# Batch 1's second FFN product by seven half products; first products in pairs; some mask products on GpSimd

## The chip, the cores and the metric

The kernel runs on one core of one Trainium2 chip. A core has five engines with queues of their own: TensorE (PE, with its weight loads PEld), VectorE (DVE), ScalarE (ACT), GpSimd (POOL) and SyncE (SP). Each works off its instructions in the order in which they were written and waits on semaphores for the others. The metric is the device time of one execution in microseconds (us). Before the change the median of three runs is 285.59 us (285.23 to 285.65); the execution that the profile shows took 285.7 us, of which its span is 284.0 us.

## What is computed

Local-global attention over 8 batches of 8 heads (head size 64), then a feed-forward block over all tokens. Each batch has 512 local and 32 global tokens.

```python
s_g = scale * q_g @ concat(k_g, k_l).T          # 32 global queries see everything
out_g = softmax(s_g) @ concat(v_g, v_l)
s_l = concat(scale * q_l @ k_g.T, where(|i - j| <= 32, scale * q_l @ k_l.T, -1e9))
out_l = softmax(s_l) @ concat(v_g, v_l)
x = concat(out_g, out_l) as (4352 tokens, 512)
h = x @ w_in            # 512 -> 2048
g = h * sigmoid(1.702 * h)
out = g @ w_out         # 2048 -> 512
```

The inputs are float32; the kernel computes with bf16 operands and float32 sums.

## The kernel before

**Work units.** A batch's 512 local tokens are a block `xL[i]`, i = 0 to 7. The global rows of all batches are gathered in `xG`, a last block of 256 rows. Two "quads" per batch, called a and c, hold four heads each on the four 32-row strips of TensorE. For each quad the code has these steps:

- `Tk`, `Tq` (L512, L316): VectorE turns the loaded k and q into the layout for TensorE; `kcopy`, `qcopy` (L504, L507) make a second, shifted copy of a part; `ext` (L538 to L545, four small copies, parts 0 to 3) puts the global rows beside them.
- `S(rnd)` (L560): TensorE makes half of the scores, round 0 or 1, into a pair of double banks that all scores share (`spair`). `X(rnd)` (L571): ScalarE takes the exponential, in two instructions of about 1000 elements. `M(rnd)` (L576): the product with the band mask, on VectorE or GpSimd.
- `U(0)`, `U(1)`, `U(2)` (L586), `Gm` (L597); together `UG`: TensorE makes the softmax sums, the two halves of the local output, and the global output, each in a bank of the pool `psP` of four banks.
- `R` (L462 to L466): VectorE turns and inverts the sums; `XL(0)`, `XL(1)` (L471) scale the local output into `xL`. `G` (L476 to L479, three small instructions) does the same for the global output into `xG`.

**First product** (512 to 2048): the block `fc`, 0 to 15, is 128 columns of `w_in`; `h_mm` makes it with four matmuls of 512 columns (L617), ScalarE's gelu (L622) takes it from its bank to `gT`. `h_step` is one `fc`. From batch 3 on `HPair(i, g)` makes the two blocks of one g (fc 2g and 2g + 1) as a 2 by 2 block product with seven half products in place of eight (L699, 14 matmuls of 256 columns), with sums of the weights (`h_weight_sums`, L660) and of the tokens (`x_sums`, L673, L674). Its steps are `m3` (a ScalarE copy of the first product), `z`, `zm`, `sub`, `add` (VectorE, L707 to L716), `inner` and `outer` (gelu).

**Second product** (2048 to 512): for batches 0 and 1 by `o_mm`, 64 matmuls of 512 columns per batch (L731). From batch 2 on by two `Pair`s per batch, seven half products each of eight matmuls of 256 columns (L800), with sums of the weights (`weight_sums`, L745: numbers 0, 3 and 4 into tiles of their own, 1 and 2 in place of parts of `w_out_sb`) and of `gT` (`g_sums`, L770, L773). Its steps have the same names as those of `HPair`: `m3` (ACT, L113), `z`, `zm`, `sub`, `add` (VectorE, L812 to L825), `evict` (ACT, L113), `store` (SP's DMAs, L838).

**Order.** The order of the work is written out by hand, engine by engine. The loop over i does, for each batch, the first product of batch i (`h_some(i)` from i = 3), and then a phase (`phase_o1` for i = 1, `phase_o(i)` for 2 to 6) in which the second product of batch i lies among the scores, exponentials, masks and outputs of batch i + 1 and the first scores of quad a of batch i + 2 (called a2, its sister c2). At the end stand the last second products and the block of the global rows. ScalarE has to load a table when it goes from gelu to exponential and back (`exp_table`, `gelu_table`, or before the first such instruction). Loads of q, k (`load`, L81, L82) and v (`load_v`, L98, L100) are issued by GpSimd's queue, the stores of results by SP's.

In `phase_o1` before the change, quad a's M(0) and M(1), c's and a2's are all on VectorE; in `phase_o` only a2's M(0) is on GpSimd.

## Time and profile before

| | |
|---|---|
| median of three runs | 285.59 us (285.23 to 285.65) |
| profiled execution | 285.7 us; its span 284.0 us |
| PE busy | 277.0 us, 98% of the span |
| DVE busy | 228.9 us, 81% |
| ACT busy | 182.1 us, 64% |
| POOL busy | 107.1 us, 38% |
| PE clock granted | 1.00 |
| L617 (first product, 128x512 matmuls) | 97.0 us busy for 432 |
| L731 (second product of batches 0 and 1) | 29.5 us busy for 128 |

The busy time of a matmul overlaps with that of the next, so rates are read from the start of one group to the start of the next. The 40 digits of an engine in the page are its busy tenths in slices of 7.1 us. The stages, by the start of their first matmul: first product of batch 0 from 17.7 us, second product of batch 0 from 31.7, first product of batch 1 from 51.0, `phase_o1` from 65.9, first product of batch 2 from 85.8, `phase_o(2)` from 99.7, `h_some(3)` from 117.3, `phase_o(3)` from 131.0, `h_some(4)` from 148.6, `phase_o(4)` from 162.3, `h_some(5)` from 180.2, `phase_o(5)` from 194.0, `h_some(6)` from 211.7, `phase_o(6)` from 225.3, `h_some(7)` from 241.7, the rest from 255.5.

### The profile page before, as it was taken

Reading aid. Unit: us, or ns where it says so; the run is one execution under the profiler, and the core shown is the slowest. Engines: PE = TensorE matmul, PEld = TensorE weight load, DVE = VectorE, ACT = ScalarE, POOL = GpSimd, SP = SyncE. Lnnn points to the kernel's source line nnn. Section 1 sums busy time; section 2 is a strip of 40 time slices with the busy share of each in tenths; the row PEclk is TensorE's granted clock in tenths of the full one; section 3 lists DMA queues with packets and bytes.
Section 4 is the critical chain, followed back from the end, with each engine's and each line's share of the span. In section 5 each row is a group of like instructions: output and inputs, shape, how many; then the busy total and the mean of one; then the engine's idle time right before and its main releaser. Section 6 shows DMA issues by size and latency. Waiting matters only on the chain.

```text
span 284.0 us, 9001 instructions
## 1 busy us (share of the span) xinstructions
PE 277.0 (98%) x3763; PEld 182.3 (64%) x3763; DVE 228.9 (81%) x518; ACT 182.1 (64%) x299; POOL 107.1 (38%) x172
## 2 busy tenths in 40 slices
PE   7899999999999999999999999999999999999994
PEld 6454445544554488746885588647875589558884
DVE  7584458986689899999989998999988898586452
ACT  4858757577778784688457873788459761873331
POOL 8993550765946001990079302960041000000001
PEclk9999999999999999999999999999999999999999
DMA  7999995899999801795039802980022003200223
GB/s 208 159 195 210 203 162 77 148 217 144 170 165 183 151 2 48 78 177 91 14 69 163 150 5 68 84 97 3 21 58 74 2 3 76 74 3 0 58 54 112
DMA packets 59352, 28.24 MB, mean 99 GB/s; under 512 B 47472, under 2 KB 49776, under 8 KB 59312
## 3 DMA queue, kind: packets, MB, share of 16 engines
q0 software_dynamic: 51760, 17.83, 56.2%
q1 hardware_dynamic: 7120, 9.18, 11.7%
q8 instruction: 29, 0.48, 0.7%
q10 hardware_dynamic: 432, 0.66, 0.7%
q14 instruction: 11, 0.09, 0.1%
HBM read 36.31 MB, written 8.91 MB: 159 GB/s over the span
## 4 chain that ended last, share of the span: by engine, by line
PE 86%; DVE 7%; DMA 2%; issue 1%; POOL 1%; ACT 1%; DVEq 0%; POOLq 0%; ACTq 0%
PE hp L617 31%; PE px L800 12%; PE op L731 10%; PE py L800 9%; PE x L800 6%; PE s L560 5%; PE ov L586 5%; PE s L699 3%; PE s L617 3%; DMA rq<-in_q_l_dram 2%; DVE gs L773 2%; DVE gs L770 1%; DVE xL L471 1%; DVE kT L512 1%; PE og L597 1%
## 5 line engine op out<-in xcount | busy, mean ns | idle before, releaser
L617 PE MATMUL hp<-xL,w_in_sb 128*128 128x512 bf16 x432 | 97.0, 379 | 0.2 <-DVE xL L471 0.2
L617 PEld LDWEIGHTS <-w_in_sb 128*128 128x128 bf16 x528 | 51.4, 98 | 51.8 <-issue 0.4
L622 ACT ACTIVATE gT<-hp 128x512 bf16<-128x512 f32 x108 | 62.7, 600 | 17.1 <-PE hp L617 16.6
L571 ACT ACTIVATE e<-s 128x1016 bf16<-128x1016 f32 (+1 forms) x56 | 53.3, 1003 | 25.7 <-PE s L560 25.7
L800 PEld LDWEIGHTS <-gs 128*128 128x128 bf16 x480 | 46.2, 98 | 6.6
L576 POOL TENSOR_TENSOR e<-e,mask 128x1760 bf16<-128x1760 bf16 x4 | 13.3, 3320 | 70.0 <-ACT e L571 70.0
L98 POOL DMA_DIRECT2D v<-in_v_l_dram x40 | 31.1, 780 | 13.6 <-PE og L597 3.8
L773 DVE TENSOR_TENSOR gs<-gT 128x512 bf16<-128x512 bf16 (+1 forms) x87 | 31.6, 398 | 3.3 <-ACT gT L622 3.3
L800 PE MATMUL py<-wsum,gs 128*128 128x256 bf16 x240 | 30.3, 273 | 0.0
L731 PE MATMUL op<-w_out_sb,gT 128*128 128x512 bf16 x128 | 29.5, 380 | 0.0
L576 DVE TENSOR_TENSOR e<-e,mask 128x1712 bf16<-128x1712 bf16 (+1 forms) x24 | 25.2, 1049 | 3.5 <-ACT e L571 3.5
L512 DVE STREAM_TRANSPOSE kT<-rk 128x512 f32<-128x512 f32 x14 | 14.5, 1037 | 12.6 <-DMA rk<-in_k_l_dram 12.6
L833 POOL DMA_DIRECT2D out_dram<-ob x2 | 1.2, 596 | 60.5 <-ACT ob L113 60.3
L731 PEld LDWEIGHTS <-gT 128*128 128x128 bf16 x128 | 11.8, 98 | 14.0
L800 PEld LDWEIGHTS <-gT 128*128 128x128 bf16 x192 | 18.0, 98 | 3.0
L800 PE MATMUL px<-w_out_sb,gT 128*128 128x256 bf16 x160 | 19.2, 273 | 0.1
L800 PE MATMUL px<-w_out_sb,gs 128*128 128x256 bf16 x160 | 19.1, 273 | 0.0
L471 DVE TENSOR_TENSOR xL<-ov,rs 128x512 bf16<-128x512 f32 x27 | 17.9, 686 | 1.0 <-PE ov L438 0.3
L113 ACT ACTIVATE ob<-px 128x512 f32<-128x512 f32 x10 | 6.0, 599 | 19.3 <-DVE zz L822 19.3
L770 DVE TENSOR_TENSOR gs<-gT 128x1024 bf16<-128x1024 bf16 (+1 forms) x29 | 17.2, 598 | 0.0
L560 PEld LDWEIGHTS <-kT 32*128 32x128 bf16 x672 | 12.5, 93 | 6.8 <-issue 5.7
L100 POOL DMA_DIRECT2D v<-in_v_g_dram x24 | 14.0, 585 | 2.2 <-DMA rq<-in_q_l_dram 1.7
(176 smaller groups left out, 429.3 us busy)
## 6 DMA issues: line engine op xcount, KB each, us to landing
out_dram<-ob SPq DMA_DIRECT2D x128, 64.0 KB, 2.7
rq<-in_q_l_dram POOLq DMA_DIRECT2D x5, 512.0 KB, 8.2
rk<-in_k_l_dram POOLq DMA_DIRECT2D x5, 512.0 KB, 10.0
v<-in_v_l_dram POOLq DMA_DIRECT2D x24, 96.0 KB, 4.8
w_in_sb<-in_moe_w_in_dram POOLq DMA_DIRECT2D x8, 256.0 KB, 6.9
w_out_sb<-in_moe_w_out_dram POOLq DMA_DIRECT2D x4, 512.0 KB, 10.1
rk<-in_k_l_dram POOLq DMA_DIRECT2D x5, 256.0 KB, 7.8
rq<-in_q_l_dram POOLq DMA_DIRECT2D x5, 256.0 KB, 7.2
```

What stands on the lines that cost most here:

```text
L98: nc.gpsimd.dma_start(out=vt[0:n, hs, c, :D], in_=vs[FIRST[c] : FIRST[c] + n, hs])
L471: nc.vector.tensor_mul(self.x[:, 2 * self.u + h, :], self.st[1 + h], self.st["rs"])
L512: nc.vector.transpose(flat[:, 0:Sl].rearrange("p (r t) -> p t r", t=16), loaded[self.b][0][:, self.u].bitcast(F32))
L560: nc.tensor.matmul(bank(self.ps, j)[:, at : at + n], lhsT=self.k[p, KEYS[c] : KEYS[c] + 128, e], rhs=qs[p, :, :, e], start=(e == 0), stop= ...
L571: nc.scalar.activation(self.E[rnd][:, 2 * i : 2 * i + 2, :n], self.ps[i][:, :, :n], AF.Exp, scale=scale)
L576: eng.tensor_mul(e, e, mask[:, rnd : rnd + 1, :n].to_broadcast([128, 4, n]))
L617: nc.tensor.matmul(hp[:, : width(i)], lhsT=w_in_c[:, fc // 4, kc, fc % 4 // 2, :, fc % 2], rhs=(xL[i] if i < B else xG)[:, kc, :], start=( ...
L622: nc.scalar.activation(out_, in_, AF.Gelu_apprx_sigmoid)
L731: nc.tensor.matmul(op, lhsT=gTs[i][:, fc, tci * 128 : tci * 128 + 128], rhs=w_out_sb[:, fc, :], start=(first and fc == 4 * f4), stop=(fc = ...
L770: nc.vector.tensor_tensor(sums[i][2][:, g, :n], t[:, g, 0, :n], t[:, g, 1, :n], ALU.add)
L773: nc.vector.tensor_tensor(sums[i][k][:, g, : n // 2], x[:, g], y[:, g], op)
L800: nc.tensor.matmul(out_, lhsT=lv[:, g, tt * 128 : tt * 128 + 128], rhs=rv[:, g, :], start=(g == 0 and k in ((1, 3, 4, 6) if self.apart els ...
```

## The change

- **Second product of batch 1.** `phase_o1` is rewritten: two `Pair`s (112 matmuls of 256 columns) in place of `o_mm` (64 of 512). The order of quads' steps among them is new. The whole second product now stands ahead of c's outputs; the first matmuls of batch 2's first product (`h_two`, new) follow after c's `UG`, a2's S(0), and among them a2's S(1).
- **Weight sums.** 0, 3 and 4 are made in four quarters each, behind the DMAs of `w_out`, during batch 0; 1 and 2 at the start of batch 1's first product. `g_sums` for batch 1 are new.
- **First product in pairs.** For batches 3 to 6 `HPair` makes g = 1 and 2 in one go (28 matmuls of 256 columns for four blocks; its vector and scalar steps are twice as wide). `h_weight_sums(2)` is new.
- **Masks.** On GpSimd are now also c's M(0) and a2's M(0) of `phase_o1`, and a2's M(1) of `phase_o(2)`, `(3)` and `(4)`.
- **Global output.** `G` is split: `keep_og` copies the bank to a tile by ScalarE, `GG` scales both quads together later on VectorE.
- **Copies.** a2's `kcopy`, `qcopy`, `ext` go to ScalarE (for batch 2 among the gelus, else inside the phase); c2's `Tk` and `Tq` stand in `phase_o` ahead of `x_sums`. S(0) of batch 2 stands one `fc` later.
- **Loads.** `load_v` of batch i + 3 is cut in two, ahead of and behind a2's M(0); `load(i + 3)` goes from the end of the phase to `h_some`, behind a2's M(1).
- **`g_sums`** of the third kind (k = 2) for g = 4 to 7 stand inside `phase_o(3)` to `(6)` in one instruction.

```diff
...
-    def load_v(b, hs=slice(0, 8)):
+    def load_v(b, hs=slice(0, 8), chunks=range(5)):
         if b == 2:
             nc.gpsimd.memset(v_view(b, 5)[:, :, :, :, D:], 1.0)
         vt = v_view(b, 5).rearrange("p u j c d -> p (u j) c d")
         vs, vg = (x[b].rearrange("h s d -> s h d") for x in (v_l, v_g))
-        for c in range(5):
+        for c in chunks:
             n = 128 if c == 2 else 96
             nc.gpsimd.dma_start(out=vt[0:n, hs, c, :D], in_=vs[FIRST[c] : FIRST[c] + n, hs])
...
+    def keep_og(q, ogs):
+        on_act(ogs[:, q.u], q.st["og"][:, : D + 2])
+
+    def GG(b, ogs):
+        rg = att.tile([128, 2, 1], F32, name="rgg")
+        nc.vector.reciprocal(rg, ogs[:, :, D : D + 1])
+        xg = att.tile([128, 2, D], BF16, name="xgg")
+        nc.vector.tensor_mul(xg, ogs[:, :, :D], rg.to_broadcast([128, 2, D]))
+        for u in range(2):
+            nc.vector.transpose(xG_by_row[:, 2 * u : 2 * u + 2, b // 4, :, b % 4],
+                                xg[:, u].rearrange("p (d h) -> p h d", h=2))
+
...
         h_act(i, fc, hp)
 
     w_h = {g: [w_in_c[:, g // 2, 2 * k : 2 * k + 2, g % 2, :, e] for e in range(2) for k in range(2)]
-           for g in (1, 4)}
-    w_s = early.bitcast(BF16).rearrange("p a b -> p (a b)")[:, : 5 * 2 * 256].rearrange(
-        "p (k u c m) -> p k u c m", k=5, u=2, c=2)
+           for g in (1, 2, 4)}
+    w_s = early.bitcast(BF16).rearrange("p a b -> p (a b)")[:, : 5 * 3 * 256].rearrange(
+        "p (k u c m) -> p k u c m", k=5, u=3, c=2)
     wh = {g: [w_s[:, k, u] for k in range(5)] for u, g in enumerate(w_h)}
...
-    def weight_sums(*ks):
+    def weight_sums(*ks, g=slice(0, FC // 2)):
         for k in ks:
             x, y, op = ((b11, b22, ALU.add), (b12, b22, ALU.subtract), (b21, b11, ALU.subtract),
                         (b11, b12, ALU.add), (b21, b22, ALU.add))[k]
-            nc.vector.tensor_tensor(wsum[k], x, y, op)
+            nc.vector.tensor_tensor(wsum[k][:, g], x[:, g], y[:, g], op)
...
         if fc == 4:
             h_weight_sums(1)
         if fc == 12:
+            h_weight_sums(2)
             h_weight_sums(4)
+    weight_sums(0, 3, 4, g=slice(2, 4))
+    weight_sums(0, 3, 4, g=slice(0, 2))
...
+    weight_sums(0, 3, 4, g=slice(4, 6))
...
+    weight_sums(0, 3, 4, g=slice(6, 8))
...
-    a.G()
-    c.G()
-    weight_sums(0, 3, 4)
-    nq[2][0].Tk()
-    nq[2][0].Tq()
-    transpose_g(4, 6)
-    nq[2][0].ext()
+    ogs = att.tile([128, 2, D + 2], F32, name="ogs", bufs=1)
+    keep_og(a, ogs)
+    keep_og(c, ogs)
+    weight_sums(1, 2)
+    GG(1, ogs)
...
     a, c = nq[2]
     for fc in range(FC):
-        if fc == 11:
-            c.Tk(False)
-            c.Tq(False)
-            c.ext((0, 1, 2))
-            c.kcopy(nc.vector.tensor_copy)
-            c.ext((3,))
-            c.qcopy(nc.vector.tensor_copy)
...
         elif fc >= 8:
             h_step(1, fc)
+        if fc == 3:
+            g_sums(1, 0, 2)
+            a.Tk(False)
+            a.Tq(False)
+            transpose_g(4, 6)
+        if fc == 6:
+            g_sums(1, 2, 4)
+            c.Tk(False)
+            c.Tq(False)
+            c.kcopy(nc.vector.tensor_copy)
+            c.qcopy(nc.vector.tensor_copy)
+            c.ext()
+        if fc == 8:
+            a.kcopy(on_act)
+        if fc == 9:
+            a.qcopy(on_act)
+        if 10 <= fc < 14:
+            a.ext((fc - 10,), on_act)
         if fc == 13:
+            g_sums(1, 4, 7, (0, 1))
+        if fc == 14:
             a.S(0)
-
-    def o_parts(i, *parts):
...
     def phase_o1():
         a, c = nq[2]
         a2, c2 = quads_of(3)
-        a2.T()
-        transpose_g(6, 8)
-        a2.ext()
+        p0, p1 = Pair(1, 0), Pair(1, 1)
+        ogs = att.tile([128, 2, D + 2], F32, name="ogs", bufs=1)
+        load_g(8, NQ)
+        load(4)
+        load_v(3, chunks=(0, 1))
+        g_sums(1, 7, 8, (0, 1))
+        p0.mm(3, 4)
+        p0.m3()
         a.X(0)
-        a.M(0)
-        loads_after(1)
-        o_parts(1, 0, 1, 2, 3, 4)
+        p0.z()
+        g_sums(1, 4, 8, (2, 3))
+        p0.mm(1, 6)
+        p0.zm()
+        p0.mm(5)
         a.S(1)
         a.X(1)
+        a2.Tk(False)
+        a.M(0)
+        p0.mm(2)
+        p0.sub()
+        p0.evict()
+        p0.mm(7)
         a.M(1)
-        o_parts(1, 5, 6, 7)
         c.S(0)
         c.X(0)
-        a.UG()
+        p0.add()
+        p0.store()
+        ov = [pbank("ov"), pbank("ov")]
+        p1.mm(3)
+        a.U(0, ov[0])
+        a.U(1, ov[1])
+        a.U(2)
         a.R()
-        c.M(0)
-        o_parts(1, 8)
+        p1.mm(4)
+        a.Gm()
+        p1.m3()
+        keep_og(a, ogs)
+        a2.kcopy(on_act)
+        c.M(0, nc.gpsimd)
+        load_v(3, chunks=(2, 3, 4))
+        a.XL(0)
+        p1.z()
+        a.XL(1)
         c.S(1)
         c.X(1)
-        a.XL(0)
-        a.XL(1)
-        a.G()
+        p1.mm(1, 6)
+        p1.zm()
+        a2.Tq(False)
+        transpose_g(6, 8)
         c.M(1)
-        o_parts(1, 9, 10, 11)
+        p1.mm(5, 2)
+        p1.sub()
+        p1.evict()
+        a2.qcopy(on_act)
+        a2.ext(copy=on_act)
+        p1.mm(7)
+        p1.add()
+        p1.store()
+        ov = [pbank(n) for n in ("ov", "og", "ov", "ov")]
+        c.U(0, ov[0])
+        c.U(1, ov[2])
+        c.U(2, ov[3])
+        c.Gm(ov[1])
         a2.S(0)
         a2.X(0)
-        c.UG()
-        loads_after(2)
         c.R()
-        a2.M(0)
+        keep_og(c, ogs)
+        a2.M(0, nc.gpsimd)
         c.XL(0)
         c.XL(1)
-        o_parts(1, 12)
-        a2.S(1)
-        a2.X(1)
+        return ogs
+
+    def h_two(ogs):
+        a, c = nq[3]
+        a2 = quads_of(4)[0]
+        pool = nc.gpsimd.tensor_copy
+        gTs[2] = moe.tile([128, FC, TB], BF16, name="gT")
+        hps = [pbank("hp") for _ in range(4)]
+        for fc in range(4):
+            h_mm(2, fc, hps[fc], (0, 1))
+        a.S(1)
+        a.X(1)
         gelu_table()
-        c.G()
-        a2.M(1)
-        o_parts(1, 13, 14, 15)
+        for kc in (2, 3):
+            for fc in range(4):
+                h_mm(2, fc, hps[fc], (kc,))
+        pt = spair()
+        for fc in range(4, 8):
+            h_mm(2, fc, bank(pt, fc - 4), range(NKC))
+        c.Tk(False)
+        c.Tq(False)
+        c.kcopy(pool)
+        c.qcopy(pool)
+        c.ext((3,), pool)
+        load_v(4)
+        load(5)
+        a2.Tk(False)
+        a2.Tq(False)
+        transpose_g(8, 10)
+        GG(2, ogs)
+        a.M(1)
+        for fc in range(4):
+            h_act(2, fc, hps[fc])
+        g_sums(2, 0, 2)
+        for n in range(2):
+            gelu(gTs[2][:, 4 + 2 * n : 6 + 2 * n, :], pt[n])
+        g_sums(2, 2, 4)
+        for fc in range(8, FC):
+            h_step(2, fc)
+            if fc in (9, 10, 12):
+                c.ext(((9, 10, 12).index(fc),), on_act)
+            if fc == 11:
+                g_sums(2, 4, 6)
+            if fc == 13:
+                g_sums(2, 6, 7)
...
         a2, c2 = quads_of(b + 1)
         p0, p1 = Pair(i, 0), Pair(i, 1)
+        ogs = att.tile([128, 2, D + 2], F32, name="ogs", bufs=1)
+        late = a2
         exp_table()
         a.UG()
         c.S(0)
         a.R()
         g_sums(i, 7, 8, (0,))
         a.XL(0)
-        g_sums(i, 7, 8, (1, 2))
+        wide = 2 < i < B - 1
+        g_sums(i, 7, 8, (1,) if wide else (1, 2))
         a.XL(1)
         g_sums(i, 7, 8, (3,))
         p0.mm(3, 4, 1)
         c.X(0)
         p0.m3()
         p0.z()
-        a.G()
+        if wide:
+            g_sums(i, 4, 8, (2,))
+        keep_og(a, ogs)
+        if late:
+            a2.kcopy(on_act)
+            a2.qcopy(on_act)
         c.M(0)
         c.S(1)
         c.X(1)
         p0.mm(6)
         p0.zm()
         c.M(1)
+        if late:
+            a2.ext(copy=on_act)
         p0.mm(5, 2)
         p0.sub()
         p0.evict()
...
         if a2:
             c.UG()
             c.R()
+            keep_og(c, ogs)
+            if i + 3 < B:
+                load_v(i + 3, chunks=(0, 1))
             a2.S(0)
             a2.X(0)
             a2.M(0, nc.gpsimd)
-            loads_after(i + 1)
+            if i + 3 < B:
+                load_v(i + 3, chunks=(2, 3, 4))
...
             c.R()
+            keep_og(c, ogs)
         c.XL(0)
         if a2:
             c.XL(1)
-            c.G()
+            GG(b, ogs)
         p1.mm(3, 4)
         p1.m3()
         p1.z()
-        if not a2:
+        if c2:
+            c2.Tk(False)
+        else:
             c.XL(1)
-            c.G()
+            GG(b, ogs)
         p1.mm(1, 6)
         p1.zm()
+        if c2:
+            c2.Tq(False)
         x_sums(i + 1)
         if a2:
             a2.S(1)
...
         p1.mm(7)
         p1.add()
         if a2:
-            a2.M(1)
+            a2.M(1, nc.gpsimd if i + 3 < B else nc.vector)
...
         for fc in range(2):
             h_mm(i, fc, hps[fc], range(NKC))
-        p = HPair(i, 1)
+        gs = (1, 2) if c else (1,)
+        fcs = iter([fc for fc in range(2, 8) if fc // 2 not in gs])
+        p = HPair(i, *gs)
         p.mm(3, 4)
         p.m3()
         for fc in range(2):
             h_act(i, fc, hps[fc])
         if c:
-            c.Tk(False)
+            if i + 3 < B:
+                load(i + 3)
             c.kcopy(pool)
-        p.z()
-        p.mm(1, 6)
-        p.zm()
-        if c:
-            c.Tq(False)
             c.qcopy(pool)
             c.ext((3,), pool)
         if a2:
             a2.Tk(False)
-            a2.kcopy(pool)
-        h_step(i, 4)
+        p.z()
+        p.mm(1, 6)
+        p.zm()
+        if a2:
+            a2.Tq(False)
+            transpose_g(2 * i + 4, 2 * i + 6)
+        h_step(i, next(fcs))
         if c:
             c.ext((0,), on_act)
-        h_step(i, 5)
+        h_step(i, next(fcs))
         p.mm(5, 2)
         p.sub()
         p.inner()
         p.mm(7)
         p.add()
-        h_step(i, 6)
-        p.outer()
-        if a2:
-            a2.Tq(False)
-            transpose_g(2 * i + 4, 2 * i + 6)
-            a2.qcopy(pool)
-            a2.ext(copy=pool)
-        if c:
-            g_sums(i, 0, 2)
-        h_step(i, 7)
-        if c:
+        if not c:
+            h_step(i, next(fcs))
+            p.outer()
+            h_step(i, next(fcs))
+        else:
+            g_sums(i, 0, 1)
+            h_step(i, 8)
+            p.outer()
+            g_sums(i, 1, 4)
+            h_step(i, 9)
             c.ext((1,), on_act)
-            g_sums(i, 2, 4)
-            for fc in range(8, 12):
-                h_step(i, fc)
-                if fc == 9:
-                    c.ext((2,), on_act)
-            g_sums(i, 4, 6)
+            h_step(i, 10)
+            c.ext((2,), on_act)
+            h_step(i, 11)
             h_step(i, 12)
             h_step(i, 13)
-            g_sums(i, 6, 7)
+            g_sums(i, 4, 7, (0, 1, 3))
             h_step(i, 14)
             h_step(i, 15)
             return
...
-    for i in range(1, B):
-        if i > 2:
-            h_some(i)
-        elif i > 1:
-            for fc in range(FC):
-                h_step(i, fc)
-                if i == 2 and fc == 0:
-                    weight_sums(1, 2)
-                if i + 1 < B:
...
-        if i == 1:
-            phase_o1()
-        elif i + 1 < B:
+    h_two(phase_o1())
+    phase_o(2)
+    for i in range(3, B):
+        h_some(i)
+        if i + 1 < B:
             phase_o(i)
...
```

More of the change, by code (lines that the diff above doesn't have):

```diff
@@ L1030 @@
             h_step(1, fc)
+        if fc == 3:
[16 more added lines that the diff above has]
+            a.ext((fc - 10,), on_act)
         if fc == 13:
+            g_sums(1, 4, 7, (0, 1))
+        if fc == 14:
             a.S(0)
-    def o_parts(i, *parts):
-        for part in parts:
-            o_mm(i, part)
-    def loads_after(i):
-        if i + 2 < B:
-            load_v(i + 2)
-        if i == 1:
-            load_g(8, NQ)
-        if i + 3 < B:
-            load(i + 3)
     def quads_of(n):
@@ L1251, in h_some @@
         g_sums(i, 6, 8, (3,))
-    for i in range(1, B):
-        if i > 2:
-            h_some(i)
-        elif i > 1:
-            for fc in range(FC):
-                h_step(i, fc)
-                if i == 2 and fc == 0:
-                    weight_sums(1, 2)
-                if i + 1 < B:
-                    c = nq[i + 1][1]
-                    if fc == 1:
-                        c.Tk()
-                        c.Tq()
-                        c.ext((3,))
-                    if fc in (3, 5, 7):
-                        c.ext(((3, 5, 7).index(fc),), on_act)
-                    if fc == 9 and i + 2 < B:
-                        a2 = quads_of(i + 2)[0]
-                        a2.T()
-                        transpose_g(2 * i + 4, 2 * i + 6)
-                        a2.ext()
-                if fc in (4, 8, 12):
-                    g_sums(i, fc // 2 - 2, fc // 2)
-                if fc == 13:
-                    g_sums(i, 6, 7)
-        if i == 1:
-            phase_o1()
-        elif i + 1 < B:
+    h_two(phase_o1())
[3 more added lines that the diff above has]
+        if i + 1 < B:
             phase_o(i)
```

## The prediction

> **What bounds the kernel now.** I read the page first: how full each engine is, slice by slice, and what the chain of work that ended last is made of.
>
> ```profile
> span 284.0 us, 9001 instructions
> PE   7899999999999999999999999999999999999994
> PEclk9999999999999999999999999999999999999999
> PE 86%; DVE 7%; DMA 2%; issue 1%; POOL 1%; ACT 1%; DVEq 0%; POOLq 0%; ACTq 0%
> L731 PE MATMUL op<-w_out_sb,gT 128*128 128x512 bf16 x128 | 29.5, 380 | 0.0
> ```
>
> TensorE is full from the third slice to the last but one at full clock, and L731, the second product that is to be replaced, has no idle time before it. So a matmul left out counts in full, and so does any wait that comes new to TensorE. Next I read the stretches of time: batch 1's second product, batch 2's first product, and batch 4's pair of stages (columns: length, then busy time and count of PE, weight loads, DVE, ACT, POOL; clock; DMA).
>
> ```profile
> 66.00:85.90 19.90, 19.90 (x370) 10.68 (x368) 15.42 (x32) 15.68 (x18) 14.41 (x21) 1.00 1.61 159
> 85.90:99.70 13.80, 13.80 (x69) 6.11 (x70) 12.73 (x31) 10.65 (x21) 3.98 (x6) 1.00 1.30 159
> 162.30:180.35 18.05, 17.91 (x394) 15.32 (x394) 16.80 (x38) 10.85 (x14) 4.78 (x4) 1.00 0.14 35
> 180.35:194.00 13.65, 13.65 (x79) 6.75 (x80) 13.33 (x28) 10.80 (x22) 8.75 (x16) 1.00 0.88 88
> ```
>
> The first stretch has no TensorE wait at all; 0.14 us of wait stands in the third. Then the chain of waits in order of time, for rates from start to start.
>
> ```profile
> 66.02 4.32 PE op L731 x20
> 85.93 13.81 PE hp L617 x64
> 101.68 1.85 PE px L800 x16
> 103.53 0.87 PE py L800 x8
> 105.95 1.75 PE px L800 x16
> 117.44 1.73 PE hp L617 x8
> 119.16 0.87 PE s L699 x8
> ```
>
> A matmul of 512 columns goes by 13.81/64 = 0.216 us, one of 256 columns by 1.75/16 = 0.109. Last, the timelines of ScalarE and VectorE, for the durations that new waits hang on, and one of GpSimd (start, duration).
>
> ```profile
> 66.67 1.28 ACT L571 ACT_TABLE_LOAD   x1
> 67.97 1.93 ACT L571 ACTIVATE e<-s 128x1016 bf16<-128x1016 f32 x2
> 103.59 0.39 ACT L113 ACTIVATE zz<-px 128x256 f32<-128x256 f32 x1
> 206.88 3.32 POOL L576 TENSOR_TENSOR e<-e,mask 128x1760 bf16<-128x1760 bf16 x1 [16.23 <-ACT e L571]
> 206.75 0.28 DVE L478 TENSOR_SCALAR xg<-og,rg 128x64 bf16<-128x64 f32 x1
> 207.23 0.41 DVE L812 TENSOR_TENSOR zz<-zz,px 128x256 f32<-128x256 f32 x1
> 208.75 1.73 DVE L673 TENSOR_TENSOR sT<-xL 128x512 bf16<-128x512 bf16 x1
> ```
>
> **The change part by part.** The span is 284.0 us and 1.7 lie around it: 285.7, 0.1 above the median of 285.59. The sum is made on 285.7. A difference below 0.2% (0.57 us) is about what a measurement of this kernel cannot tell from no change.
>
> *Fewer matmuls in `phase_o1`.* 64 matmuls of 512 columns go: their pieces in the chain, from the start of each to the next piece, come to 4.32 + 3 x 2.70 + 2 x 0.97 = 14.36 (over 64 x 0.216 = 13.82 by the starts between other work). 112 of 256 come; a whole `Pair` of 56 reads 1.85 + 0.87 + 0.98 + 1.75 + 0.87 = 6.32 off the chain, two are 12.65 with rounding. **-1.71.**
>
> *First products in pairs (batches 3 to 6).* One g more per batch is made by halves: 8 matmuls of 512 columns (1.73 in the chain) become 14 of 256, 14 x 0.109 = 1.53. Four times -0.20 is **-0.8**. The vector steps of `HPair` get twice as wide (128x256 takes 0.41 and 128x512 0.68 now; at most 2 x 0.68 = 1.36 for 128x1024); z, zm and sub each have 8 to 14 matmuls beside them (0.87 and more), so I take nothing for them, and up to 0.3 a batch for the range. In batch 4 VectorE is late today: two `g_sums` of L773 take 1.98 us at 156.71, while GpSimd copies for a2, against 0.40 each elsewhere, and the chain runs through VectorE up to 164.4. Batch 4's period, 148.6 to 180.2, is 31.6 against batch 3's 31.3. a2's small copies now leave GpSimd for ScalarE: **-0.2** (0 to -0.3).
>
> *Weight sums and other moved work.* Each of 0, 3 and 4 is 1.20 us; in quarters 12 x about 0.35 (a quarter is 512 columns a partition, like L770's 0.41 at most) of VectorE. VectorE is idle for 7.34 us up to 32.19 and 1.90 up to 37.88, waiting for k; three quarters and `h_weight_sums(2)` (5 x 0.36, from L660's 1.09 for three) fit there. The last quarter comes behind the last of `w_out` and a's M(0), up to 0.35 ahead of VectorE's next work. Taken: **0**, range 0 to 0.35. Without that cover the 3.5 + 1.8 us would delay batch 0's scores.
>
> *ScalarE's copies in batch 1's first product.* `kcopy`, `qcopy`, `ext` of a now stand between gelus; two small ones take 0.52 at 34.84 on ScalarE, and S(0) waits for the last, `ext(3)`, behind fc 13's gelu: **+0.1**.
>
> *New waits in `phase_o1` and `h_two`.* Here the order is new, and the trace of before has no such wait, so I walk each engine's instructions in their new order with the durations above. T is the end of the last matmul of batch 1's first product (about 66.1).
>
> (A) a's S(1) needs the banks that X(0) reads. ScalarE now has `m3` first, which waits for both `mm(3, 4)`: T + 1.75; then 0.39, the table 1.28 and X(0) with start-up 2.0: T + 5.4. TensorE until then has `mm(1, 6)` and `mm(5)`: 40 x 0.109, T + 4.37. It waits **1.04**. Before, the table started at 66.67, right behind the last gelu.
> (B) c's U(2) takes the bank that `evict` frees; `zm`, a's M(1) (1.05 on VectorE) and `sub` stand ahead of it: **0.27**.
> (C) a2's S(0) needs `ext(3)`, which on ScalarE stands behind X(1), `evict`, `qcopy` and three copies (0.60 + 0.39 + 4 x 0.2 to 0.3): **0.7**.
> (D) the first `hp` banks of batch 2 come free by `XL(0)`, `XL(1)` and `keep_og(c)`. R and XL take 3.1 us (sT 0.71 to XL 1.29, with 0.25 and 0.71 between), while c's `Gm` and a2's S(0) give 0.16 + 0.58 and two `hp` 0.43 each: **0.3**; `keep_og` stands behind a2's X(0), 1.93 + 0.25: **0.5**.
> Small ones on banks: 0.15.
>
> Together 1.04 + 0.27 + 0.7 + 0.3 + 0.5 + 0.15 = **+3.0**. No row has the copies on ScalarE of 128x192 f32, 128x384 bf16, 128x66 f32; they lie between 0.26 (half of the two small ones) and 0.60 (L113, 128x512 f32). With 0.26 throughout, and A as it is, 2.3; with 0.60 for the three wide ones 3.6. I take 3.0, by 0.39, the nearest row (128x256 f32). The matmuls of batch 2 that are now cut by kc have a few more starts: **+0.2** (0 to 0.3).
>
> *Masks on GpSimd.* 3.32 us there for 1.05 on VectorE. c's M(0) in `phase_o1` ends about T + 13.8 and its U needs it at T + 16.9; a2's M(0) and M(1) are needed 10 us later, a phase's a2 M(1) ends about 24.5 us into the phase and is read at 31. Hidden: **0**. What they do to VectorE shows in L673's row: the first of `x_sums` takes 1.73 beside the 3.32 of GpSimd, where its median is 0.41.
>
> *Loads.* Two `load_v` chunks with their v_g, four issues on GpSimd (L98 780 ns, L100 585: 2 x 0.78 + 2 x 0.59 = 2.7), now stand ahead of M(0) in i = 2, 3, 4; M(0) is needed 10 us later. Three chunks stand behind it and land in 4.8, a phase before use. `load(i + 3)`, two issues more, goes out behind M(1), 25 us into the period, lands by 10.0 and is read 15 us after that; `load(4)` and `load_g` go ahead of the v chunks. SP's stores keep their order behind `add`. **0**; without that slack up to 2.7 once.
>
> *`phase_o`.* z, U(2) and the first `hp` bank each stand a little later behind ScalarE's new copies (`keep_og` 0.29, `kcopy`, `qcopy`, 0.3 to 0.5 each) in five phases: **+0.1**, range 0 to 1.5 (0.3 a phase). `GG`'s four instructions replace two times three small ones (0.16, 0.28, 0.32), and its product of 128 elements a partition lies between 0.28 and 0.41 (L478, L812): nothing.
>
> Sum: -1.71 - 0.8 - 0.2 + 0.1 + 3.0 + 0.2 + 0.1 = **+0.7**; 285.7 + 0.7 = **286.4**, +0.3% against the median 285.59. With the waits at 2.3 to 3.6 and up to 0.3 for the rest its own range is 285.7 to 287.3.
>
> **The rivals.** *Wait A does not come (not slower).* If ScalarE loads its table while it still waits for `mm(3, 4)`, X(0) ends 1.28 earlier, at T + 4.1, before TensorE is done at T + 4.37, and 1.04 goes: 285.4. With the other waits at their lower bound (0.7 less) it is 284.7. The result is no longer slower from 0.25 us of missing waits on, and faster from 1.4. For it: the table at 66.67 needed nothing but the gelu ahead of it, and the +3.0 is walked from durations, not seen in a trace. Against it: ScalarE works in order, and the table stands behind `m3`. Range 284.6 to 285.9.
>
> *GpSimd's mask gets ahead of `GG` (slower).* While GpSimd's 3.32 us mask ran from 206.88, L812, with one operand in the matmul banks, took its usual 0.41; L673, with both operands in SBUF, took 1.73 up to the mask's end (median 0.41). `GG`'s product has both operands in SBUF; L478, which it replaces, read the bank and began at 206.75, 0.13 us before the mask. In `phase_o(5)`, where no loads stand ahead of the mask, it begins at about that moment again. If the mask is first, the product waits up to 3.3, `z` behind it is as late, and TensorE waits for `mm(5, 2)`, less the `mm(1, 6)` beside it of 0.87 that is left: 3.3 - 0.9 = 2.4; 286.4 + 2.4 = 288.8. For it: L673's row; against it: a matter of 0.1 us, in one phase of five.
>
> The Trainium skill ("SBUF — State Buffer", section "SBUF: two separate sides") states a rule that gives this case: VectorE and GpSimd share a pair of ports as an exclusive lock, which the one that starts first holds for its whole instruction, and among VectorE's operations one with two SBUF inputs is concerned. The trace's 1.73 for 0.41 agrees. By the rule, with the mask first, the sum would be 288.8; by L478's row it stays 286.4.
>
> *The halves of the first product save nothing.* If the doubled vector steps of `HPair` are late by 0.2 a batch, the -0.8 goes, and 0.1 more in the phase behind: 287.3. For it: in batch 4 the chain runs through VectorE for 9 us. Against it: 28 matmuls leave each step twice the time.
>
> **How the numbers follow.** My forecast has 0.46, the missing wait 0.34, GpSimd's mask 0.14, nothing saved 0.06. Faster by over 0.2% is below 285.0: two thirds of the second case, whose terms could all be smaller, 0.22. Within 0.2% is 285.0 to 286.2: the rest of the second, 0.12, and the lower edge of the first, 0.08: 0.20. Slower: 0.38 + 0.14 + 0.06 = 0.58. The range goes from the low end of the second case, 284.6, to the third, 288.8.
>
> **What would show it.** Right: in `phase_o1` a TensorE idle time of about 1 us ahead of L560, ended by ScalarE's exponential, and shorter ones ahead of U, a2's S(0) and the first `hp`; from the first matmul of the second product to the first of batch 2's first product 1 us more than the 19.9 of before; the first product's stages of batches 3 to 6 shorter by 0.2 each; the quarter sums inside VectorE's idle time. Wrong: X(0) starting before T + 3, no wait ahead of a's S(1); `GG`'s product over 3 us in `phase_o(5)`; vector steps of `HPair` that end TensorE's waits.

## The result and the profile after

The changed kernel takes 286.55 us (median of six executions, 286.17 to 287.23) against 285.60 us before (285.23 to 285.70): a ratio of 1.0039, 95% interval 1.0024 to 1.0053. It is slower by 0.95 us. The profiled execution took 286.17 us, its span is 284.5 us. The page (busy tenths in slices of 7.1 us, and the chain by engine):

```profile
span 284.5 us, 9136 instructions
PE   7899999998989999999999999999999999999994
PE 68%; ACT 1%; issue 0%; DVE 0%
```

Where TensorE's row had nines throughout there are now two eights, in the slices from 64 and from 78 us. ScalarE's share of the chain is 1% as before, but it now stands in these stages, from 83.31 us on (shown below). The same four stretches as before, shifted to the stages of this execution (columns: length, then busy time and count of PE, weight loads, DVE, ACT, POOL; clock; DMA):

```profile
65.60:85.85 20.25, 18.68 (x394) 15.26 (x393) 15.61 (x28) 13.02 (x21) 14.10 (x16) 1.00 1.55 156
85.85:101.30 15.45, 14.78 (x94) 6.50 (x94) 12.97 (x29) 13.48 (x23) 12.91 (x15) 1.00 0.84 76
163.50:181.25 17.75, 17.73 (x393) 15.23 (x394) 17.21 (x34) 12.60 (x22) 7.25 (x7) 1.00 0.34 48
181.25:194.60 13.35, 13.27 (x78) 7.24 (x81) 11.30 (x21) 10.64 (x20) 6.65 (x8) 1.00 0.60 69
```

TensorE's busy time in the first stretch fell from 19.90 to 18.68 us, part of it because one S moved into the second. But 1.57 us of waits are new there, and 0.67 in the second; batch 4 (the last two rows) takes 31.10 us from its first U to the next batch's, 31.58 before. So the change is two effects of opposite sign. From the start of batch 1's second product to batch 2's first outputs (the first U of `phase_o(2)`) I call it the stretch: 33.81 us before (65.86 to 99.67), 35.70 after (65.58 to 101.28), **+1.89**. The four periods from there to the first U of `phase_o(6)`, 125.54 us before (99.67 to 225.21), are 124.39 now (101.28 to 225.67), **-1.15**. Batch 1's first product up to there takes 15.02 instead of 14.84 us, **+0.18**. The sum is +0.92, beside +0.95 between the medians. The two spans differ by only 0.5 us, because this execution began 0.46 us earlier: its first scores waited 1.0 us for q, those of the one shown before 1.5 us.

TensorE's waits in the changed kernel (total, times, longest):

```profile
PE s L357 <- DVE q L316: 1.0, 2, 0.8
PE s L560 <- ACT e L571: 0.7, 1, 0.7
PE s L560 <- ACT kT L113: 0.6, 1, 0.6
PE hp L629 <- DVE xL L471: 0.5, 2, 0.4
PE hp L629 <- ACT ogs L113: 0.3, 1, 0.3
```

The four lower ones are a's S(1) behind X(0), a2's S(0) behind `ext(3)`, and the `hp` banks behind `XL` and behind `keep_og`: A, C and D of the prediction. Of the 0.5 us behind `XL` only 0.36 is new; 0.16 stands in batch 1's first product, where the kernel before had it too. TensorE's timeline at these places:

```profile
69.07 1.09 PE L812 MATMUL px<-w_out_sb,gs 128*128 128x256 bf16 x8
71.20 0.27 PE L560 MATMUL s<-qc,kT 32*128 32x108 bf16 x6 [0.69 <-ACT e L571]
71.76 1.05 PE L812 MATMUL px<-w_out_sb,gs 128*128 128x256 bf16 x8
84.32 0.35 PE L597 MATMUL og<-v,e 128*32 128x66 bf16 x20
85.23 0.53 PE L560 MATMUL s<-q,kT 32*128 32x160 bf16 x16 [0.57 <-ACT kT L113]
86.56 1.19 PE L629 MATMUL hp<-xL,w_in_sb 128*128 128x512 bf16 x4 [0.36 <-DVE xL L471]
88.01 0.59 PE L629 MATMUL hp<-xL,w_in_sb 128*128 128x512 bf16 x2 [0.26 <-ACT ogs L113]
```

ScalarE's timeline at A and the chain at C and D:

```profile
67.53 0.38 ACT L113 ACTIVATE zz<-px 128x256 f32<-128x256 f32 x1 [1.15 <-PE px L812]
67.93 1.28 ACT L571 ACT_TABLE_LOAD   x1
69.22 1.93 ACT L571 ACTIVATE e<-s 128x1016 bf16<-128x1016 f32 x2
```

```profile
83.31 0.60 ACT ob L113
83.90 0.41 ACT qc L113
84.32 0.41 ACT q L113 x2
84.72 0.15 ACT qc L113
84.88 0.31 ACT kT L113
85.19 0.05 issue
85.23 0.70 PE s L560 x20
85.93 1.91 ACT e L571 x2
87.84 0.13 ACT ogs L113
```

The table load stands still until `m3` (L113, zz) has run, and X(0) behind it; the last gelu had ended at 66.38. At the other end the copies for a2 run behind `evict` (ob) although what they read was ready at 81.7, and then S(0), X(0) and `keep_og` follow each other in line, with only six of the first product's matmuls beside them.

### The profile page after: what moved, and what is told of

Its sections match the earlier page's. It is cut to its first block, busy times and chain, and to the rows that moved or that the text cites. A ratio compares the mean times of both kernels' runs of the same rounds, so it can differ in the third digit from the quotient of the medians.

```text
span 284.5 us, 9136 instructions
## 1 busy us (share of the span) xinstructions
PE 274.4 (96%) x3815; PEld 189.5 (67%) x3835; DVE 232.5 (82%) x494; ACT 190.2 (67%) x339; POOL 118.4 (42%) x162
## 4 chain that ended last, share of the span: by engine, by line
PE 68%; ACT 1%; issue 0%; DVE 0%
PE hp L629 24%; PE px L812 13%; PE py L812 9%; PE x L812 6%; PE s L711 5%; PE s L560 4%; PE ov L586 4%; PE s L629 1%; ACT e L571 1%; PE og L597 1%; PE s L586 0%; ACT ob L113 0%; ACT qc L113 0%; DVE ob L1424 0%; ACT q L113 0%
## 5 line engine op out<-in xcount | busy, mean ns | idle before, releaser
L629 PE MATMUL hp<-xL,w_in_sb 128*128 128x512 bf16 x370 | 85.9, 379 | 1.5 <-DVE xL L471 0.5
L634 ACT ACTIVATE gT<-hp 128x512 bf16<-128x512 f32 x96 | 54.5, 604 | 9.6 <-PE hp L629 9.1
L812 PEld LDWEIGHTS <-gs 128*128 128x128 bf16 x560 | 53.9, 98 | 7.8 <-DVE gs L782 0.2
L576 POOL TENSOR_TENSOR e<-e,mask 128x1760 bf16<-128x1760 bf16 (+1 forms) x9 | 29.8, 3310 | 26.2 <-ACT e L571 26.1
L785 DVE TENSOR_TENSOR gs<-gT 128x256 bf16<-128x256 bf16 (+3 forms) x86 | 32.6, 409 | 7.7 <-ACT gT L634 7.5
L812 PE MATMUL py<-wsum,gs 128*128 128x256 bf16 x288 | 36.2, 273 | 0.1
L812 PEld LDWEIGHTS <-gT 128*128 128x128 bf16 x224 | 20.9, 98 | 3.7
L113 ACT ACTIVATE ob<-px 128x512 f32<-128x512 f32 x12 | 7.2, 599 | 20.3 <-DVE zz L834 20.3
L634 ACT ACTIVATE gT<-s 128x1024 bf16<-128x1024 f32 (+1 forms) x12 | 11.2, 957 | 11.3 <-DVE ob L725 6.8
L782 DVE TENSOR_TENSOR gs<-gT 128x1024 bf16<-128x1024 bf16 (+3 forms) x24 | 18.5, 772 | 0.0
L560 PE MATMUL s<-q,kT 32*128 32x160 bf16 (+1 forms) x448 | 14.9, 246 | 0.7 <-ACT kT L113 0.6
```

The costliest lines, as they stand in the source:

```text
L560: nc.tensor.matmul(bank(self.ps, j)[:, at : at + n], lhsT=self.k[p, KEYS[c] : KEYS[c] + 128, e], rhs=qs[p, :, :, e], start=(e == 0), stop= ...
L576: eng.tensor_mul(e, e, mask[:, rnd : rnd + 1, :n].to_broadcast([128, 4, n]))
L629: nc.tensor.matmul(hp[:, : width(i)], lhsT=w_in_c[:, fc // 4, kc, fc % 4 // 2, :, fc % 2], rhs=(xL[i] if i < B else xG)[:, kc, :], start=( ...
L634: nc.scalar.activation(out_, in_, AF.Gelu_apprx_sigmoid)
L782: nc.vector.tensor_tensor(sums[i][2][:, g, :n], t[:, g, 0, :n], t[:, g, 1, :n], ALU.add)
L785: nc.vector.tensor_tensor(sums[i][k][:, g, : n // 2], x[:, g], y[:, g], op)
```

## The experiments

A table first. Stretch and periods are from the starts of matmuls in each profile; "before" is the median of the runs of the kernel before on the same chip.

| kernel | us, median (n) | before | ratio, 95% | stretch | four periods |
|---|---|---|---|---|---|
| before, profile above | 285.60 (6) | | | 33.81 | 125.54 |
| the change | 286.55 (6) | 285.60 | 1.0039 (1.0024 to 1.0053) | 35.70 | 124.39 |
| a0: the change again | 286.40 (9) | 285.43 | 1.0033 (1.002 to 1.0046) | 35.70 | 124.39 |
| e1: pairs alone | 284.15 (5) | 285.69 | 0.9955 (0.9942 to 0.9967) | 33.81 | 124.40 |
| e1 again | 284.40 (9) | 285.67 | 0.9951 (0.9931 to 0.9971) | 33.81 | 124.39 |
| e2: m3 on VectorE | 285.41 (11) | 285.69 | 0.9992 (0.998 to 1.0005) | 34.69 | 124.44 |
| e3: copies first | 285.50 (11) | 285.69 | 1.0004 (0.9987 to 1.002) | 34.86 | 124.40 |
| e4: one pair | 287.96 (5) | 285.69 | 1.0081 (1.0068 to 1.0094) | 35.71 | 125.53 |
| e5: e2 and e3 | 285.10 (11) | 285.43 | 0.9992 (0.9978 to 1.0005) | 33.83 | 124.46 |
| e6: sums ahead | 285.02 (12) | 285.43 | 0.9984 (0.9969 to 0.9999) | 34.54, 33.86 | 124.38 |
| e7: mask first | 289.15 (4) | 285.43 | 1.0142 (1.0112 to 1.0171) | 35.71 | 126.69 |
| e8: Gm first | 285.04 (12) | 285.67 | 0.9968 (0.9951 to 0.9985) | 33.35, 34.06 | 124.38 |

**The second half of the change alone.** `phase_o1` (with `o_mm`) and batch 2's first product, here `h_two`, as they were before, all from `phase_o(2)` on as changed:

```diff
...
-    h_two(phase_o1())
+    phase_o1()
+    h_two()
     phase_o(2)
```

> The part from batch 3's first product on alone: phase_o, h_some, GG and the loads as changed, batch 1's second product and batch 2's first product as before the change. My theory: the change is two effects of opposite sign, about -1.2 us from batch 2's phase on and about +1.9 us in phase_o1 and h_two; this kernel keeps only the first, so 284.3 to 284.8 against 285.6 before (ratio 0.996 to 0.998), with periods of 31.1 us between the first outputs of two batches against 31.3 to 31.4. Rival: the shorter periods depend on the new phase_o1 (on what it puts on other engines); then no gain here, 285.4 to 285.9.

The stretch is back at 33.81 and the periods stay at 31.10, so they owe nothing to the new `phase_o1`. The time, 284.15, is a little below what I expected. The two stages of the stretch in this kernel's windows:

```profile
65.60:85.50 19.90, 19.74 (x367) 10.64 (x369) 15.38 (x32) 15.55 (x18) 14.29 (x21) 1.00 1.68 169
85.50:99.40 13.90, 13.79 (x64) 6.17 (x65) 12.93 (x28) 10.78 (x21) 4.11 (x7) 1.00 1.27 148
```

This kernel is faster than both: 0.9955 of the time before, and 0.9951 in a second measurement on another chip.

> e1_pairs_alone once more, on the same chip as e8_gm_first: 284.0 to 284.7, stretch 33.81 us, periods 31.1 us. If e8_gm_first is at or below it, batch 1's second product by halves pays once its waits are gone; if e8_gm_first is above it by 0.3 us or more, it does not pay in any order tried here.

**Is it the order on ScalarE (A)?**

```diff
-        p0.m3()
+        p0.m3("dve")
```

> The changed kernel with one edit: p0.m3 of phase_o1 on VectorE, so that ScalarE's table load and X(0) no longer stand behind both mm(3, 4). Theory: a's S(1) waits for X(0), which stands behind m3 and the table load; the wait ahead of a's S(1) (0.69 us shown, 1.26 us more than its matmuls need) goes, X(0) starts at about 67.7 us instead of 69.2, and the time falls by 0.9 to 1.3 us, to 285.3 to 285.6. Rival: what is won is waited for again behind it (c's U(2), a2's S(0), the first hp banks hang on VectorE's chain); then less than 0.4 us comes off.

The stretch falls by 1.01 us, the time by 1.1, to 285.41. ScalarE's timeline shows why: the table is loaded right behind the last gelu.

```profile
66.98 1.28 ACT L571 ACT_TABLE_LOAD   x1
68.27 1.93 ACT L571 ACTIVATE e<-s 128x1016 bf16<-128x1016 f32 x2
```

This execution ran 0.58 us later up to there than the one of the change, so X(0) starts 1.53 us earlier in the stretch. Of A's 1.26 us 1.07 is gone and 0.19 is left; C, D and the rest behind it stay as they were within 0.1 us, so nothing is waited for again.

**Is it the order of the copies (C and D)?**

```diff
         p1.sub()
-        p1.evict()
         a2.qcopy(on_act)
         a2.ext(copy=on_act)
+        p1.evict()
...
         a2.S(0)
+        keep_og(c, ogs)
         a2.X(0)
         c.R()
-        keep_og(c, ogs)
```

> The changed kernel with two moves on ScalarE in phase_o1: a2's qcopy and ext ahead of p1's evict, and keep_og(c) ahead of a2's X(0). Theory: a2's S(0) waits 0.6 us for ext(3) behind evict, and the fourth hp bank 0.26 us for keep_og(c); both waits go, but VectorE's R and XL (end at about 87.1 us) do not get earlier, so the first hp banks wait longer: of the 1.3 us that these places lose, about 0.5 us comes off, 286.0 to 286.2. Rival 1: the waits are independent and add up, 0.8 to 1.3 us comes off. Rival 2: ext(3) is not what S(0) waits for, nothing changes (286.4 to 286.7).

The wait ahead of a2's S(0) is gone, and that behind `keep_og`; the stretch falls by 0.84. That is inside rival 1's 0.8 to 1.3 and not my 0.5. S(0) starts 0.63 us earlier in the stretch, and from its start to a's S(1) it is 3.08 us instead of 3.30: the waits for XL grew, as expected, but by less than I had reckoned. The time fell by 1.05 between the medians; the 0.2 beyond the stretch is less than the starts differ.

**Both.** The two edits together:

> The changed kernel with both edits: p0.m3 on VectorE, and on ScalarE a2's copies ahead of p1's evict and keep_og(c) ahead of a2's X(0). Each alone shortened the stretch from the second product of batch 1 to batch 2's first outputs, 35.70 us in the changed kernel, by 1.01 and 0.84 us. Theory: the two waits are apart and add up, 33.85 us, as long as the stretch of before (33.81) with the periods of the changed kernel: 284.4 to 284.8. Rival: VectorE's chain carries one into the other, and one gain is lost (285.2 to 285.6).

They add up: 33.83, as long as before the change. The time, 285.10, is above what I expected. In the profiled execution (285.12 us) a wait at the start explains 0.75 us (waits, then VectorE's timeline):

```profile
PE s L560 <- ACT q L113: 0.8, 1, 0.8
```

```profile
29.08 1.10 DVE L757 TENSOR_TENSOR wsum<-w_out_sb 128x512 bf16<-128x512 bf16 x3 [3.10 <-DMA w_out_sb<-in_moe_w_out_dram]
34.07 1.04 DVE L512 STREAM_TRANSPOSE kT<-rk 128x512 f32<-128x512 f32 x1 [1.38 <-DMA rk<-in_k_l_dram]
```

The quarter sums (L757) began at 27.49 in the profile of the change and at 29.08 here, since `w_out` landed later; k followed later as well, and a's S(0) of batch 1 waited 0.75 us. It was k's own landing that made this wait and not the sums ahead of `Tk`: VectorE was done with them and idle for 1.38 us until k came (34.07, against 32.48 in the change). Whether the other executions started as late isn't recorded.

**Do pairs give what the count of matmuls says?** One g by halves in batches 3 to 6, as before the change, all else changed:

```diff
-        gs = (1, 2) if c else (1,)
+        gs = (1,)
...
-            g_sums(i, 0, 1)
+            h_step(i, next(fcs))
+            p.outer()
+            g_sums(i, 0, 2)
+            h_step(i, next(fcs))
+            g_sums(i, 2, 4)
             h_step(i, 8)
-            p.outer()
-            g_sums(i, 1, 4)
```

> The changed kernel with HPair for one g alone in batches 3 to 6 (as before the change), all else as changed. Theory: a g by halves saves 8 x 0.216 - 14 x 0.109 = 0.20 us a batch, so this kernel is 0.8 us slower than the changed one, 287.2 to 287.5, and its periods are 31.3 us against 31.1. Rival: the wide vector steps eat the saving, the time stays at 286.5; or the other edits of the phase bear the gain.

The periods are 31.29, 31.35, 31.37 and 31.52 us against 31.10, 31.10, 31.10 and 31.09 of the change: 0.19, 0.25, 0.27 and 0.43 more, 1.14 together. Before the change they were 31.31, 31.34, 31.58 and 31.31, almost the same sum (125.54 and 125.53), but not the same parts. The first difference is the matmul count, 0.20. In the third period, batch 4's, this kernel with one pair is 0.21 us shorter than before: the wait that stood there left with the other edits, as the prediction has it, and not with the second pair (which edit took it away isn't separated). The fourth is 0.21 longer than before: in batch 6's first product the matmuls between the pair's two groups take 1.86 us for 1.73 and its last six 0.74 for 0.66, short waits of this kernel alone. That the two cancel in the sum is chance. In the chain of the changed kernel the two groups of a pair product are:

```profile
120.76 1.75 PE s L711 x16
124.23 1.31 PE s L711 x12
```

28 matmuls in 3.06 us, with no wait among them. The medians differ by 1.4 us, more than the periods do, and the time is above the 287.2 to 287.5 expected; what makes up the rest isn't shown.

**The rival with the mask.** GG's small reciprocal four times for batch 6, to let GpSimd's mask start first:

```diff
-        nc.vector.reciprocal(rg, ogs[:, :, D : D + 1])
+        for _ in range(4 if b == 6 else 1):
+            nc.vector.reciprocal(rg, ogs[:, :, D : D + 1])
```

> The changed kernel with GG's small reciprocal four times for batch 6 instead of once (0.5 us of VectorE), so that in phase_o(5) its product comes behind the start of GpSimd's mask of a2, not 0.13 us ahead of it as the profile of the changed kernel shows (207.41 against 207.54). Theory (the rival of the prediction, by L673's row and the 1.03 us of the same product under the mask in h_two): the product takes over 3 us, until the mask ends, mm(5, 2) or the pair of batch 6 behind it waits, and the time rises by 2.4 us or, through x_sums behind it, somewhat more, 288.5 to 290. Rival: the product runs beside the mask, it costs the 0.5 us of VectorE at most, under 287.2.

In the changed kernel GG's product (L613) starts 0.13 us before the mask and takes 0.29 us; in `h_two`, where it starts under a mask that runs from 87.92 to 91.25, it takes until 0.14 us after the mask's end:

```profile
207.54 3.35 POOL L576 TENSOR_TENSOR e<-e,mask 128x1760 bf16<-128x1760 bf16 x1 [19.62 <-ACT e L571]
207.41 0.29 DVE L613 TENSOR_TENSOR xgg<-ogs,rgg 128x128 bf16<-128x128 f32 x1
87.92 3.33 POOL L576 TENSOR_TENSOR e<-e,mask 128x1760 bf16<-128x1760 bf16 x1 [4.55 <-ACT e L571]
90.36 1.03 DVE L613 TENSOR_TENSOR xgg<-ogs,rgg 128x128 bf16<-128x128 f32 x1
```

With 0.6 us of small work ahead of it (GpSimd's, VectorE's and TensorE's timelines of this kernel):

```profile
208.29 3.32 POOL L576 TENSOR_TENSOR e<-e,mask 128x1760 bf16<-128x1760 bf16 x1 [19.61 <-ACT e L571]
208.76 3.00 DVE L614 TENSOR_TENSOR xgg<-ogs,rgg 128x128 bf16<-128x128 f32 x1
212.57 1.91 PE L813 MATMUL px<-w_out_sb,gs 128*128 128x256 bf16 x16 [2.22 <-DVE zz L825]
```

The product takes 3.00 us for 0.29 and ends 0.15 us after the mask, z is late, TensorE waits 2.22 us for it, the period is 33.38 us and the time 289.15, 2.75 above the changed kernel on the same chip (a0, below). In the changed kernel L824 (z), with one operand in the matmul banks, took 0.43 under the mask at 208.03. The Trainium skill ("SBUF — State Buffer", section "SBUF: two separate sides") says that a VectorE instruction with two SBUF inputs and a GpSimd instruction that reads SBUF block each other in full, the later one until the earlier ends. The trace agrees with it in both places.

> The changed kernel unedited, for the comparison on the same chip: 286.2 to 287, the stretch from batch 1's second product to batch 2's first outputs 35.7 us and the periods 31.1 us as in its first profile, whatever the first scores wait for q at the start.

Stretch and periods are those of the first profile, at a start that is 0.6 us later.

**A better order for the halves?** e5, and c's U(0) and U(1) ahead of p1's last product, so that VectorE's R can start sooner; then the same with c's Gm back ahead of a2's S(0) (e8). The edit of e6 against e5:

```diff
         p1.mm(1, 6)
-        p1.zm()
         a2.Tq(False)
         transpose_g(6, 8)
+        p1.zm()
...
-        p1.mm(7)
-        p1.add()
-        p1.store()
         ov = [pbank(n) for n in ("ov", "og", "ov", "ov")]
         c.U(0, ov[0])
         c.U(1, ov[2])
+        p1.mm(7)
+        c.R()
+        p1.add()
+        p1.store()
         c.U(2, ov[3])
-        c.Gm(ov[1])
         a2.S(0)
+        c.Gm(ov[1])
...
         a2.X(0)
-        c.R()
```

> As e5_both, and c's U(0) and U(1) ahead of p1's last product, c's R ahead of p1's add, a2's Tq in VectorE's idle time ahead of zm, a2's S(0) ahead of c's Gm. Theory: what is left of the waits ahead of batch 2's first matmuls (about 0.3 on XL, 0.2 on evict ahead of U(2)) comes from VectorE's R and XL, which begin only behind p1's add; they end some 0.9 us earlier, and the stretch falls to 33.3 to 33.5 us, below that of before: 283.9 to 284.3, ahead of pairs alone or level with it. Rival: sub or add or U(2) waits in their place, 284.4 to 285.

> e6_sums_ahead once more, for one look: if the 0.64 us in U(0) was a chance of that execution the stretch is 33.9 us; if it belongs to the kernel (something that U(0) waits for in this place) it is 34.5 us again.

> As e6_sums_ahead, with c's Gm back ahead of a2's S(0), so that keep_og(c) is done before S(0) and X(0) starts behind S(0) at once. Theory: in e6_sums_ahead the stretch was 34.54 us, with 0.64 us in which c's U(0) stood still while TensorE waited for nothing that the profile shows, and 0.4 us of a's S(1) waiting for X(0); the second goes by this order, and if the first was a chance of that execution the stretch is 33.4 to 33.6 us and the time 284.0 to 284.4. Rival: the standstill in U(0) comes back, then 34.1 to 34.3 us and 284.6 to 285.

> e8_gm_first once more for one look. Its twelve executions lay in two groups, 283.9 to 284.4 and 285.0 to 286.0 us, and its profile was one of the first. Theory: in the second group TensorE stands still once or twice for 0.5 to 0.65 us at a place that changes, as in the two profiles of e6_sums_ahead (in U(0), and in a second product of batch 2); a profile of 285 us or more would show such standstills beside the same stretch of 33.35 us. Rival: the difference is the start (the first scores wait for q, 0 to 1.9 us in the profiles here), or one of the waits of phase_o1.

e6 gave 34.54 us and a time of 285.02, a miss, with a standstill in U(0). In its second profile (285.46 us) that one was not there (33.86), but another one in a product of batch 2. e8 reached 33.35, 0.46 below the kernel before, in an execution of 284.10 us; its second profile, of an execution of 285.11 us, shows a standstill again, in a's S(1), at a start 0.29 us later. The three, each from its own profile:

```profile
82.27 0.32 PE L586 MATMUL ov<-e,ones 128*32 128x192 bf16 x8 [0.64 <-issue]
```

```profile
108.11 0.39 PE L812 MATMUL px<-w_out_sb,gs 128*128 128x256 bf16 x2 [0.48 <-issue]
```

```profile
87.68 0.42 PE L560 MATMUL s<-q,kT 32*128 32x228 bf16 x12 [0.51 <-issue]
```

"issue" means that the profile shows nothing that TensorE waits for. From start to start a's S(1) and its successor lie 1.17 us apart instead of 0.48; with the later start that is 0.98 of the 1.01 us by which this execution of e8 is longer than the other.

The packets of the traces show more. TensorE's own instructions come by DMA as well (the page's line of that queue: transfers, MB, share):

```profile
q8 instruction: 30, 0.49, 0.7%
```

Each of the 30 transfers has 16384 bytes; for some 7700 recorded instructions (a weight load and its matmul are two) that is about 256 each. Counted in order, the three standstills begin at instructions 2241 (e6), 3009 (e6 again) and 2497 (e8), 256 or 512 apart: at borders between the instructions of two transfers. Pair the transfers in order with such borders, 256 apart: the 14 traces then have 403 borders, and at none did TensorE go on earlier than 2.31 us after the start of its transfer. At 398 it got there 2.34 us after that start or later, and there is no such pause. At the other five it got there after 1.44, 1.59, 1.73, 2.05 and 2.10 us; the first three are the standstills above, the last two are pauses of about 0.2 us in the second profile of e6. So, as far as traces can show it, TensorE waited there for its next instructions. Why these transfers started late stays open, and no run here moves one by an edit.

e8's twelve executions go from 283.88 to 285.96 us, e1's fourteen from 284.11 to 284.71. So in this order the halves do win in TensorE's work, in the execution without a standstill. But over twelve executions e8's median, 285.04, is 0.64 above e1's 284.40 on the same chip: by the mark set beforehand (0.3 us) the second product by halves does not pay in any order tried. Whether all of e8's longer executions have such standstills isn't recorded.

## Why the prediction was right

The forecast was 286.4 us, the time is 286.55. The forecast stood on 285.7 and the median before is now 285.60, so the change itself is +0.95 where +0.7 was forecast. Its steps, in us, from start to start of matmuls:

| step | predicted | measured |
|---|---|---|
| 112 matmuls for 64 | -1.71 | -1.72 |
| first products in pairs, and batch 4's wait | -1.0 | -1.15 |
| S(0) behind `ext(3)` | +0.1 | +0.18 |
| A, a's S(1) behind X(0) | +1.04 | +1.26 |
| B, c's U(2) behind `evict` | +0.27 | +0.26 |
| C, a2's S(0) behind `ext(3)` | +0.7 | +0.64 |
| D, `hp` behind XL; behind `keep_og` | +0.3; +0.5 | +0.32; +0.58 |
| small ones on banks | +0.15 | +0.44 |
| more starts in `h_two` | +0.2 | +0.11 |
| `phase_o` | +0.1 | 0 |
| sum | +0.7 | +0.92 |

How the right column is read: the matmuls of the two `Pair`s take 12.62 us from start to start, without the waits; the 64 before took 14.34. A is from the start of `mm(5)` at 69.07 to that of `mm(2)` at 71.76, 2.69, less 0.87 and 0.56 for the work in it. B is 1.36 for c's U, less the 1.10 of before. C is 0.91 from c's Gm (84.32) to S(0) (85.23), less 0.27 for Gm. D is 0.75 for two matmuls and 1.45 for four, less 0.216 each. The small ones are c's S(0) (0.72 for 0.57), a's U and Gm (1.48 for 1.37) and c's S(1) (0.74 for 0.56); what each of them waits for isn't shown. `h_two`'s 64 matmuls take 14.91 us, 13.90 before, and 0.90 of the difference is D. The groups of matmuls in `phase_o` keep their lengths within 0.1 us, but for batch 4's wait. The waits together are 3.5 us, predicted 3.0, inside the 2.3 to 3.6. The column's sum is that of the stages.

- *Mechanism.* e2 takes out most of A by giving one copy to another engine, e3 takes out C with a part of D by order alone, and together they bring the stretch to 33.83: that the new waits cost what the halves save is shown, not only argued. A and the small ones were taken too small; B, C and D came within 0.1 us.
- *Some of the closeness is luck.* The waits came out 0.5 us above their term, the pairs, `h_two` and `phase_o` 0.34 below theirs.
- *One sign did not come.* From the first matmul of the second product to the first of batch 2's first product there should have been 1 us more than the 19.9 of before. It is 20.23 for 19.91, 0.32 more. The prediction's own terms don't give 1 us there: D lies behind that point, and a2's S(1), 0.56 us, had moved behind it. The sign was set wrong, not the sum.
- *The pairs' term, with batch 4's wait, was too small by 0.15.* By period the change saves 0.21, 0.24, 0.48 and 0.22 us. Beyond the matmul count of 0.20 each that is 0.28 in batch 4's period, where 0.2 was taken, and 0.07 in the other three.
- *Hidden work.* The quarter sums stood in VectorE's idle time, from 27.49 and 30.00 on and again at 36.28, behind k's first landing; the last ones came behind M(0) at 41.77. The masks and loads on GpSimd let no matmul wait in the profile. But one cover is thin: the next point.
- *The rival with the mask* did not decide, by 0.13 us in `phase_o(5)`. Its price, predicted as 2.4 us, is 2.22 in TensorE's wait and 2.75 in the time.
- *Wait A doesn't come* was wrong: the table load stood behind `m3` on ScalarE, 67.93 behind 67.53. *Nothing saved* was wrong as well.

What stays open: why the transfers ahead of the standstills started late, and how much later `w_out` would have to land before the sums ahead of `Tk` reach S(0).

## What to carry to other kernels

A product by halves saves an eighth of the multiplications but adds an in-order chain of copies, sums and evictions on two other engines; where a table change, a bank or a copy for the next stage stands in that chain, the order of the queue decides whether anything is left. Here 1.72 us of saved matmuls met 3.5 us of waits, of which two moves on ScalarE and one copy given to VectorE took back 1.9. Take a change with parts in different stages apart by stage: half of this one was worth 0.45%, and the whole cost 0.39%.

## What was not expected

- The first scores wait for q between less than 0.2 and 1.9 us from one profile to the next, and 0.7 and 1.7 us in two profiles of one kernel (e8); a difference of spans of two single profiles can be off by as much. The length of the stretch repeats to 0.05 us (the change's was 35.70 in two profiles, e1's 33.81 in two) where no standstill lies in it.
- TensorE stood still for 0.48, 0.64 and 0.51 us at three different places in three of the four profiles of e6 and e8, and in none of the others for more than 0.2 us. The profile's waits name no cause; its packets do: all three are borders at which the transfer of TensorE's next instructions had started late.
- GG's product of 128 elements a partition took 0.29, 1.03 and 3.00 us: free, 0.9 us before GpSimd's mask ended, and 0.5 us after the mask began.
